# The begin of a one-core attention and MLP kernel: which engine issues the first loads, and in which order

## The chip, the cores and the metric

The kernel runs on one core of one Trainium2 chip. The metric is the device time of one execution in microseconds (us), the median over several runs. The profile of one execution stands beside it: a record of every instruction on the engines PE (TensorE: matmul products; PEld is its weight loads), DVE (VectorE), ACT (ScalarE), POOL (GpSimd) and SP (SyncE), and of every packet that the core's 16 DMA engines move. Transfers are issued by SP and ACT into hardware queues (q1 is SP's, q10 ACT's) and by POOL into a software queue (q0).

## What is computed

The reference is a linear attention with decay, followed by a two-layer MLP. `lam` holds eight numbers, one for each head.

```python
# q, k, v: (4, 8, 768, 64) float32; lam: (8,); block = 64
for b in range(nb):
    intra = (qb @ kb.T * Dmask) @ vb           # Dmask[i, j] = lam ** (i - j) for i >= j, else 0
    inter = (qb * lam_pow) @ kv_state
    out[:, :, sl] = intra + inter
    kv_state = lam_block * kv_state + (kb * rev_pow).T @ vb
x = out.transpose(0, 2, 1, 3).reshape(3072, 512)
h = x @ w_in                                    # w_in (512, 2048)
result = (h - tanh(h)) @ w_out                  # w_out (2048, 512)
```

The weights w_in and w_out come in with eight bytes for each number (the kernel sees them as I64) and are rounded to float32 on the chip.

## The kernel before

The sequence is cut into six groups of 128 positions, `g` = 0 to 5, and each group has one **chunk** for each of the four batches: chunk 0 to chunk 3 of group 0 are what the begin works on. A chunk's q, k and v are 256 KB each, 128 positions by 8 heads by 64 numbers, so a row in DRAM that lies together is 256 bytes. `load_natural` (L174, the transfers at L190) issues them.

The weight w_in is read in 16 **blocks** of 512 KB, `raw64`, (u, i) with u the quarter of the hidden layer and i the slice of 128 inputs. `load_weights` (L275) issues the loads into four buffers (`WAHEAD`), `weights` (L285) rounds a block: three ScalarE instructions (L353, L354, L355) read the raw block, and two of VectorE (L357, L358) finish it. When the third ScalarE instruction is done, the buffer is free for the block four places later. Blocks with i = 2 or 3 are loaded as two halves of 64 partitions (L271), the others as one transfer (L266).

The work of group 0 on a chunk b is, in order:

- `att_transpose` (L392): four transposes of q and four of k on TensorE, each set copied from PSUM by ScalarE (L394) as `qt` and `kt`.
- `att_scores` (L408): sixteen products `sp` of kt and qt; VectorE multiplies them by the decay mask `whole` (L415) into `ss`.
- `first_out` (L459): the products `op` of v and `ss`. For the chunks 0 and 1 together, and for 2 and 3 together, ScalarE then copies the tokens `xt` (L466, `first_tokens`).
- `att_decay` (L438): VectorE scales the chunk's k in place; `kv_products` (L447): the products for the running state.

`up_plain` (L903) then yields the products `h` of the MLP's first layer, from xt and a rounded block, four products at a step of the generator. `steps(unit, 2)` runs two steps, those of one block for 256 tokens.

The mask `whole` needs lam: `few` (L97) loads the eight numbers, VectorE widens them (L129), TensorE transposes them into `rows` (L132), VectorE copies them to `lam_all` (L133) and makes the mask by eight scans (L121). `idle_products(n)` (L105) writes n products of a zero tile that nobody reads: fillers that keep TensorE at work. Each of them shows as two passes in the profile, as does every product of this kernel.

The order of the begin is written out by hand, and `tc.keep_in_program_order` pins it on each engine. SP issues q of all four chunks, v of the chunks 0 and 1 and the blocks 1, 2 and 3; ACT issues k of the chunks 0 and 1; POOL issues lam, block 0, and k and v of the chunks 2 and 3. Two of POOL's transfers are held: `held(op, engine)` makes the next transfer of that engine wait for an instruction `op`. Block 0 waits for a scan of the mask (`begun`), and v of chunk 2 for the masked scores of chunk 0. From block 4 on, SP issues w_in, each block when its buffer is free.

Of the kernel before, what the change touches and what calls it, by code (L numbers as in the profile page):

```python
# [24 lines left out]
def kernel(  # L25
# [32 lines left out]
    nc = tc.nc  # L58
    B, H, S, D = q.shape
# [3 lines left out]
    KI = DM // 128  # L63
# [3 lines left out]
    NU = DFF // 512  # L67
# [26 lines left out]
    fwd = const.tile([128, NP, BLK], F32)  # L94
    nc.vector.memset(fwd[:, 0, :], 0.0)
    few = const.tile([H, 1], F32, name="few")
    nc.gpsimd.dma_start(out=few, in_=bass.AP(tensor=lam.tensor, offset=lam.offset, ap=[[1, H], [1, 1]]))  # L97
    make_identity(nc, ident)

    idle = psum.tile([128, 512], F32, name="idle", tag="w", bufs=1)  # L100
# [1 line left out]
    def idle_products(n, first=False):  # L102

        for _ in range(n):
            op = nc.tensor.matmul(out=idle[:, 0:128], lhsT=fwd[:, 0, :], rhs=fwd[:, 0, :], start=True, stop=True)  # L105
            if not first:
                tc.keep_in_program_order(op)
# [20 lines left out]
    few_wide = xpool.tile([H, BLK], F32, name="few_wide", tag="xt1")  # L128
    tc.keep_in_program_order(nc.vector.tensor_copy(few_wide, few.to_broadcast([H, BLK])))  # L129
    rows = psum.tile([128, 512], F32, name="rows", tag="z", bufs=1)[:, 0:H]  # L130
    idle_products(8, True)
    tc.keep_in_program_order(nc.tensor.transpose(out=rows, in_=few_wide, identity=ident[0:H, 0:H]))  # L132
    tc.keep_in_program_order(nc.vector.tensor_copy(lam_all, rows))  # L133


    begun = scans(range(NP), ident)
# [37 lines left out]
    def load_natural(g, b, names):  # L174
        for name, src, bufs in (("q", q, 2), ("k", k, 3), ("v", v, 4)):
            if name in names:
                if (g, b, name) in ((0, 2, "q"), (0, 3, "q"), (0, 3, "k")):
                    x = opool.tile([128, H, D], F32, name=f"{name}_nat", tag="o")
                else:
                    x = (qpool if name == "q" else io).tile([128, H, D], F32, name=f"{name}_nat", tag=name, bufs=bufs)  # L180
                rows = src[b, :, ts(g, BLK), :].rearrange("h s d -> s h d")
                if name == "q":
                    parts = [(nc.sync, x, rows)]
                elif g == 0:
                    parts = [(nc.gpsimd if b > 1 else nc.scalar if name == "k" else nc.sync, x, rows)]
                else:
                    parts = [(nc.sync, x[ts(1 - t, HALF), 4:8], rows[ts(t, HALF), 4:8]) for t in range(2)]
                    parts.insert(0, (nc.sync, x[:, 0:4], rows[:, 0:4]))
                for eng, to, of in parts:
                    op = tc.keep_in_program_order(eng.dma_start(out=to, in_=of))  # L190
                    if begin.get(eng) is not None:
                        wait_for(op, begin.pop(eng))
                raw[g, b][name] = x
# [67 lines left out]
    def load_block(eng, dst, kind, n, m, first=False):  # L261

        if kind == "out":
            tied(first, eng.dma_start(out=dst, in_=moe_w_out[ts(m * KH + n, 128), :].rearrange("k (a n) -> k a n", a=2)))
        elif m < 2:
            op = tied(first, eng.dma_start(out=dst, in_=w_in_u[ts(m, 128), :, ts(n, 256)]))  # L266
            if begin.get(eng) is not None:
                wait_for(op, begin.pop(eng))
        else:
            for j in range(2):  # L270
                op = tied(first, eng.dma_start(out=dst[ts(1 - j, 64)], in_=w_in_u[ts(2 * m + j, 64), :, ts(n, 256)]))  # L271
                if begin.get(eng) is not None:
                    wait_for(op, begin.pop(eng))

    def load_weights(n):  # L275

        while ready["loaded"] < min(n, ready["may"]):
            if moe_w_in.dtype != F32:
                raw64 = stage.tile([128, 2, 256], I64, name="raw64", tag="raw64", bufs=WAHEAD)
                block = blocks[ready["loaded"]]  # L280
                load_block(nc.gpsimd if ready["loaded"] in (0, *range(NU * KI, NU * KI + 4)) else nc.sync, raw64, *block, True)
                wraw[ready["loaded"]] = raw64
            ready["loaded"] += 1

    def weights(n):  # L285

        while ready["done"] < min(n, len(blocks)):
            at_ = ready["done"]
            load_weights(at_ + WAHEAD)
            kind, n_, m = blocks[at_]  # L290
            if kind == "out" and m == 0:
                pair[n_] = pair_tiles(n_)
            w = w1[n_][:, m] if kind == "in" else pair[n_][m][:, 0:2]
            if at_ in wraw:
                round_block(w, wraw.pop(at_), at_ < 3 * KI)
            else:
                load_block(nc.gpsimd, w, kind, n_, m)
            ready["done"] += 1
# [102 lines left out]
    def att_scores(g, bs):  # L401
        for b in bs:
            qt, kt, _ = tr[g, b]
            if g == 0:
                sp = [bank("sp", "att", 4).rearrange("s (p i) -> s p i", p=NP) for _ in range(2)]
                for p in range(NP):
                    for j in range(2):
                        tied(True, nc.tensor.matmul(out=sp[j][:, p, :], lhsT=kt[ts(j, 64), p, :],  # L408
                                                    rhs=qt[ts(j, 64), p, :], start=True, stop=True))
                if b % 2 == 0:  # L410
                    sc[0, "half"] = wst.tile([128, 8, 256], F32, name="ss", tag="w").rearrange(
                        "s (b j x) c -> s b j (x c)", b=2, j=2).rearrange("s b j (p i) -> s b j p i", p=NP)
                ss = sc[0, "half"][:, b % 2]
                for j in range(2):
                    op = tied(True, nc.vector.tensor_tensor(ss[:, j], sp[j], whole[:, j], op=AL.mult))  # L415
                sc[g, b] = ss
                continue

            sp = [bank("sp", "att", 4)[:, 0:6 * HALF].rearrange("s (x i) -> s x i", x=6) for _ in range(2)]
            for p in (0, 2, 1, 3):  # L420
                x, r = p % 2, p // 2
                for j in range(2):
                    kj, qj = kt[ts(j, 64), p, :], qt[ts(j, 64), p, :]

                    k0, k1 = (kj[:, ts(t if r == 0 or g >= GB else 1 - t, HALF)] for t in range(2))
                    tied(g != 1, nc.tensor.matmul(out=sp[j][ts(r, HALF), x:3 + p:2 + p - x, :], lhsT=k0,  # L426
                                                  rhs=qj.rearrange("d (t i) -> d t i", t=2), start=True, stop=True))
                    tied(g != 1, nc.tensor.matmul(out=sp[j][ts(1 - r, HALF), 2 + p, :], lhsT=k1,  # L428
                                                  rhs=qj[:, HALF:BLK], start=True, stop=True))
            ss = work.tile([128, 2, 6, HALF], F32, name="ss", tag="ss")  # L430
            for j in range(2):
                op = tied(g != 1, nc.vector.tensor_tensor(ss[:, j], sp[j], mask[:, j], op=AL.mult))
            sc[g, b] = ss
        return op

    def att_decay(g, b):
        kp = raw[g, b]["k"].rearrange("s (p j) d -> s p j d", j=2)
        return tied(g != 1, nc.vector.tensor_tensor(kp, kp, bwd if g > 0 else bwd_first, op=AL.mult))  # L438
# [525 lines left out]
    def steps(it, n):  # L964
        for _ in range(n):
            next(it)


    def held(op, *engines):
        begin.clear()  # L970
        begin.update({eng: op for eng in engines})

    def more_raw(n):
        ready["may"] = n
        load_weights(n)

    held(begun, nc.gpsimd)
    more_raw(1)
    more_raw(2)
    load_natural(0, 2, "q")  # L980
    more_raw(3)
    load_natural(0, 2, "k")
    att_transpose(0, (0,))
    idle_products(4)
    held(att_scores(0, (0,)), nc.gpsimd)
    load_natural(0, 2, "v")
    load_natural(0, 3, "qkv")
    more_raw(4)
    ready["may"] = len(blocks)
    att_decay(0, 0)  # L990
    idle_products(1)
    att_transpose(0, (1,))
    idle_products(4)
    att_scores(0, (1,))
    first_out(0)
    weights(1)
    att_decay(0, 1)
    idle_products(5)
    first_out(1)
    first_tokens(0)  # L1000
    idle_products(2)
    att_transpose(0, (2,))
    weights(2)
    unit = up_plain(0, [(i, c + 10 * a) for c in (11, 12) for i in range(KI) for a in range(2)])
    steps(unit, 2)
    att_scores(0, (2,))
    kv = kv_products(0, (0, 1))
    weights(3)
    att_decay(0, 2)
    att_transpose(0, (3,))  # L1010
    steps(unit, 2)
    first_out(2)
    weights(4)
    att_scores(0, (3,))
    att_decay(0, 3)
    steps(unit, 2)
    first_out(3)
    first_tokens(1)
    first_state((0, 1), kv)
# [185 lines left out]
```

## Time and profile before

| What | Value |
|---|---|
| median of 3 runs | 658.95 us (658.14 to 660.87) |
| profiled execution, its own time | 660.13 us |
| its span, from the first to the last instruction | 658.3 us |
| PE busy | 649.2 us (99%) |
| DVE busy | 471.1 us (72%) |
| ACT busy | 244.4 us (37%) |
| POOL busy | 204.9 us (31%) |
| DMA moved | 125.78 MB, mean 191 GB/s |
| issue to landing: q of chunk 0, lam, block 0 | 4.1 us, 5.3 us, 8.3 us |

The span is 1.8 us shorter than the execution's own time. The profile's views name a group of instructions by its line in the kernel, its engine, its operation and the tiles that it writes and reads. The timeline merges neighbours of one kind into a row: start, duration, engine, line, operation, tiles, shape, count, and in brackets how long the engine had been idle before and who ended the wait. The table by stages gives for each stretch of time how long each engine was busy. The DMA view gives for a stretch the packets and megabytes of each queue, and the median time from an issue to its landing.

### The profile page before, as it was taken

What the parts mean: (1) busy time and instruction counts of PE and PEld (TensorE: products, weight loads), DVE (VectorE), ACT (ScalarE), POOL (GpSimd) and SP (SyncE); (2) the same over time, 40 slices, a digit from 0 to 9 for tenths busy, and PEclk for the clock granted to TensorE, in tenths of its full rate; (3) what the DMA queues carried; (4) which work ended last, traced back from release to release, by engine and by line L of the source; (5) the groups of instructions that cost most, each with busy time, mean ns of one, the idle gap of its engine ahead of it and who ended that gap; (6) DMA issues with size and microseconds to landing.
All of it is one profiled execution on the core that took longest, in us unless ns stands there. A gap on an engine that the chain in (4) does not pass through costs nothing. (4 is left out here: it accounts for less than half of the span.)

```text
span 658.3 us, 14826 instructions
## 1 busy us (share of the span) xinstructions
PE 649.2 (99%) x5761; PEld 595.1 (90%) x5761; DVE 471.1 (72%) x895; ACT 244.4 (37%) x485; POOL 204.9 (31%) x353
## 2 busy tenths in 40 slices
PE   8999999999999999999999999999999999999998
PEld 7788888888888999988989988999998899998897
DVE  3556989968878895678786658798468697466663
ACT  2676964722321223532213443213353223263210
POOL 3000125777123335202334401244411254400241
PEclk9999999999999999999999999999999999999999
DMA  9929976996759758957656966676967476721274
GB/s 207 226 95 203 261 225 208 374 295 197 198 119 232 222 183 247 221 107 175 196 188 195 249 127 151 148 237 207 244 129 147 128 245 224 228 75 32 88 245 165
DMA packets 156215, 125.78 MB, mean 191 GB/s; under 512 B 126977, under 2 KB 129281, under 8 KB 156145
## 3 DMA queue, kind: packets, MB, share of 16 engines
q0 software_dynamic: 27056, 88.04, 43.1%
q1 hardware_dynamic: 127008, 36.27, 26.3%
q8 instruction: 46, 0.75, 0.5%
q10 hardware_dynamic: 2080, 0.52, 0.4%
q14 instruction: 25, 0.20, 0.1%
HBM read 103.81 MB, written 20.97 MB: 190 GB/s over the span
## 5 line engine op out<-in xcount | busy, mean ns | idle before, releaser
L752 POOL DMA_DIRECT2D wb<-fine x148 | 79.8, 539 | 190.9 <-PE y L794 66.8
L851 ACT ACTIVATE q<-y 128x128 f32<-128x128 f32 x96 | 26.6, 277 | 142.8 <-PE y L847 141.8
L847 PE MATMUL y<-wb,g 128*128 128x128 f32 x456 | 60.4, 277 | 0.0
L903 PE MATMUL h<-xt,w 128*128 128x256 f32 x256 | 58.3, 383 | 0.3 <-DVE w L358 0.3
L847 PEld LDWEIGHTS y<-wb,g 128*128 128x128 f32 x456 | 55.1, 192 | 0.9 <-issue 0.2
L903 PEld LDWEIGHTS h<-xt,w 128*128 128x128 f32 x256 | 47.4, 190 | 7.9 <-DVE w L358 1.3
L617 ACT ACTIVATE th<-g 128x512 f32<-128x512 f32 x40 | 25.2, 630 | 66.6 <-DVE g L635 50.7
L755 POOL DMA_DIRECT2D wb<-factors x44 | 23.7, 541 | 83.1 <-PE y L794 50.8
L609 PE MATMUL y<-xt,w 128*128 128x256 f32 x192 | 45.0, 379 | 0.0
L618 DVE TENSOR_TENSOR g<-g,th 128x512 f32<-128x512 f32 x40 | 27.6, 691 | 20.7 <-ACT th L617 20.7
L609 PEld LDWEIGHTS y<-xt,w 128*128 128x128 f32 x192 | 36.4, 190 | 5.1 <-ACT g L626 0.2
L847 PE MATMUL zw<-wb,g 128*128 128x128 f32 x304 | 40.3, 275 | 0.0
L609 PE MATMUL y<-tt,ws 128*128 128x256 f32 x160 | 37.8, 379 | 0.0
L609 PE MATMUL y<-tt,w 128*128 128x256 f32 x160 | 37.8, 379 | 0.0
L609 PE MATMUL z<-xt,ws 128*128 128x256 f32 x160 | 37.8, 379 | 0.0
L794 PE MATMUL y<-wb,g 128*128 128x256 f32 x160 | 37.3, 379 | 0.0
L847 PEld LDWEIGHTS zw<-wb,g 128*128 128x128 f32 x304 | 37.0, 192 | 0.2 <-DVE g L853 0.2
L794 PE MATMUL w<-wb,g 128*128 128x256 f32 x160 | 35.4, 379 | 0.0
L794 PEld LDWEIGHTS w<-wb,g 128*128 128x128 f32 x160 | 30.4, 190 | 4.1
L609 PEld LDWEIGHTS z<-xt,ws 128*128 128x128 f32 x160 | 30.4, 190 | 4.1
L794 PEld LDWEIGHTS y<-wb,g 128*128 128x128 f32 x160 | 30.4, 190 | 4.1
L609 PEld LDWEIGHTS y<-tt,w 128*128 128x128 f32 x160 | 30.3, 190 | 4.2
(217 smaller groups left out, 1465.9 us busy)
## 6 DMA issues: line engine op xcount, KB each, us to landing
wb<-fine POOLq DMA_DIRECT2D x148, 256.0 KB, 3.6
wb<-factors POOLq DMA_DIRECT2D x44, 256.0 KB, 4.5
wb<-fine_in POOLq DMA_DIRECT2D x36, 256.0 KB, 4.4
raw<-in_moe_w_out_dram SPq DMA_DIRECT2D x12, 512.0 KB, 5.4
rest<-fine POOLq DMA_DIRECT2D x20, 256.0 KB, 4.5
raw<-in_moe_w_in_dram SPq DMA_DIRECT2D x16, 256.0 KB, 7.5
fine<-f POOLq DMA_DIRECT2D x16, 256.0 KB, 5.0
q_blk<-in_q_dram SPq DMA_DIRECT2D x128, 32.0 KB, 3.2
```

The costliest lines, as they stand in the source:

```text
L609: nc.tensor.matmul(out=t[:, m, :], lhsT=wt[:, kt, ts(m, 128)], rhs=x[:, kt, :], start=first and m == 0 and kt == 0, stop=kt == 1, skip_gro ...
L617: nc.scalar.activation(th, src, AF.Tanh)
L618: nc.vector.tensor_tensor(dst(c), src, th, op=AL.subtract)
L752: nc.gpsimd.dma_start(out=t.rearrange("p m c -> p (m c)"), in_=fine[TWICE.index(n_), SUB.index(x_)].rearrange("p u c -> p (u c)"))
L755: nc.gpsimd.dma_start(out=t, in_=factors[XAT[FACT[n_][1]]][:, 2 * x_:2 * x_ + 2, :])
L794: nc.tensor.matmul(out=t[:, m, :], lhsT=a[:, u, kt, ts(m, 128)], rhs=wb[:, kt, :], start=first and u == 0 and m == 0 and kt == 0, stop=u = ...
L847: tied(x == STEPS[-1], nc.tensor.matmul(out=dst, lhsT=a[:, u, :], rhs=wb[:, ts(u, 128)], start=x in (1, 2) and u == 0, stop=u == NU - 1, s ...
L851: nc.scalar.activation(keep, dst, AF.Copy)
L903: tied(u == 0, nc.tensor.matmul(out=hm[c][:, m, :], lhsT=w1[u][:, i, a, ts(m, 128)], rhs=xt[0, t][:, i, :], start=m == 0 and i == 0, stop= ...
```

## The change

`few` is loaded by ScalarE, ahead of its two loads of k. Both holds are gone. POOL issues the first four blocks of w_in instead of block 0 alone (`range(KI)`, KI is 4), and between them k and v of the chunks 2 and 3, all written ahead of the first transposes. SP keeps q of all chunks, and v of the chunks 0 and 1. The fillers are divided anew: 6 before `rows` and 3 behind it instead of 8 before; none instead of 1 behind the first scores; 3 instead of 5 and 3 instead of 2 around the second `first_out`; 3 new ones ahead of the last. The first two steps of `up_plain` move ahead of the transposes of chunk 2, block 1 is rounded ahead of those, `kv_products` stands later, and block 3 is rounded behind the scores of chunk 3.

```diff
-    nc.gpsimd.dma_start(out=few, in_=bass.AP(tensor=lam.tensor, ...
+    nc.scalar.dma_start(out=few, in_=bass.AP(tensor=lam.tensor, ...
...
-    idle_products(8, True)
+    idle_products(6, True)
     tc.keep_in_program_order(nc.tensor.transpose(out=rows, in_=few_wide, identity=ident[0:H, 0:H]))
     tc.keep_in_program_order(nc.vector.tensor_copy(lam_all, rows))
+    idle_products(3)
...
-                load_block(nc.gpsimd if ready["loaded"] in (0, *range(NU * KI, NU * KI + 4)) else nc.sync, raw64, *block, True)
+                load_block(nc.gpsimd if ready["loaded"] in (*range(KI), *range(NU * KI, NU * KI + 4)) else nc.sync, raw64, *block, True)
...
-    held(begun, nc.gpsimd)
-    more_raw(1)
     more_raw(2)
-    load_natural(0, 2, "q")
+    load_natural(0, 2, "qk")
     more_raw(3)
-    load_natural(0, 2, "k")
+    load_natural(0, 2, "v")
+    load_natural(0, 3, "qk")
+    more_raw(4)
+    load_natural(0, 3, "v")
+    ready["may"] = len(blocks)
     att_transpose(0, (0,))
     idle_products(4)
-    held(att_scores(0, (0,)), nc.gpsimd)
-    load_natural(0, 2, "v")
-    load_natural(0, 3, "qkv")
-    more_raw(4)
-    ready["may"] = len(blocks)
+    att_scores(0, (0,))
     att_decay(0, 0)
-    idle_products(1)
     att_transpose(0, (1,))
     idle_products(4)
     att_scores(0, (1,))
     first_out(0)
     weights(1)
     att_decay(0, 1)
-    idle_products(5)
+    idle_products(3)
     first_out(1)
     first_tokens(0)
-    idle_products(2)
-    att_transpose(0, (2,))
-    weights(2)
+    idle_products(3)
     unit = up_plain(0, [(i, c + 10 * a) for c in (11, 12) for i in range(KI) for a in range(2)])
     steps(unit, 2)
+    weights(2)
+    att_transpose(0, (2,))
+    steps(unit, 2)
     att_scores(0, (2,))
-    kv = kv_products(0, (0, 1))
     weights(3)
     att_decay(0, 2)
+    kv = kv_products(0, (0, 1))
     att_transpose(0, (3,))
     steps(unit, 2)
     first_out(2)
-    weights(4)
     att_scores(0, (3,))
+    weights(4)
     att_decay(0, 3)
-    steps(unit, 2)
+    idle_products(3)
     first_out(3)
```

More of the change, by code (lines that the diff above doesn't have):

```diff
@@ L96 @@
     few = const.tile([H, 1], F32, name="few")
-    nc.gpsimd.dma_start(out=few, in_=bass.AP(tensor=lam.tensor, offset=lam.offset, ap=[[1, H], [1, 1]]))
+    nc.scalar.dma_start(out=few, in_=bass.AP(tensor=lam.tensor, offset=lam.offset, ap=[[1, H], [1, 1]]))
     make_identity(nc, ident)
@@ L1012 @@
     first_out(2)
+    att_scores(0, (3,))
     weights(4)
-    att_scores(0, (3,))
     att_decay(0, 3)
-    steps(unit, 2)
+    idle_products(3)
     first_out(3)
```

## The prediction

> **What bounds the kernel now.** I read the page first: its busy table and the PE row of the 40 slices.
>
> ```profile
> span 658.3 us, 14826 instructions
> ...
> PE 649.2 (99%) x5761; PEld 595.1 (90%) x5761; DVE 471.1 (72%) x895; ACT 244.4 (37%) x485; POOL 204.9 (31%) x353
> ...
> PE   8999999999999999999999999999999999999998
> ```
>
> TensorE is idle for only 9.1 us in all. The change touches the first 35 us alone, so I ask how far it shifts one marker: the end of the last L459 product of chunk 3. Next, the table by stages tells whether a shift lasts:
>
> ```profile
> 34.20:60.00 25.80, 25.80 (x145) 22.22 (x146) 13.34 (x24) 18.60 (x32) 0.00 (x0) 1.00 0.59 132
> 60.00:80.00 20.00, 19.74 (x182) 16.60 (x181) 19.18 (x45) 16.71 (x32) 2.28 (x4) 1.00 1.03 248
> ```
>
> The first two numbers behind each stretch are its length and PE's busy time: after the marker PE does not wait, so what is won or lost before it reaches the end. Third, the timeline of the begin (start, duration, engine, line; in brackets the idle time before):
>
> ```profile
> 1.06 3.78 PE L105 MATMUL idle<-fwd 128*128 128x128 f32 x16 [1.06 <-DVE fwd L95]
> 1.26 0.66 POOL L97 DMA_DIRECT2D few<-in_lam_dram  x1 [0.82 <-POOLq L1189]
> ...
> 6.94 0.24 PE L132 MATMUL rows<-ident,few_wide 8*128 8x8 f32 x1 [2.10 <-DVE few_wide L129]
> ...
> 8.02 1.06 PE L392 MATMUL tp<-ident,k_nat 128*128 128x128 f32 x4
> 8.22 0.76 POOL L266 DMA_DIRECT2D raw<-in_moe_w_in_dram  x1 [5.72 <-DVE whole L121]
> ...
> 10.71 2.08 PE L408 MATMUL sp<-qt,kt 64*128 64x128 f32 x16
> ...
> 14.91 1.16 PE L408 MATMUL sp<-qt,kt 64*128 64x128 f32 x16
> ...
> 18.34 1.09 PE L459 MATMUL op<-ss,v_nat 128*64 128x128 f32 x16
> ...
> 20.78 1.89 PE L903 MATMUL h<-xt,w 128*128 128x256 f32 x8
> ...
> 26.77 0.63 PE L392 MATMUL tp<-ident,k_nat 128*128 128x128 f32 x4 [1.33 <-DMA k_nat<-in_k_dram]
> ...
> 33.10 1.09 PE L459 MATMUL op<-ss,v_nat 128*64 128x128 f32 x16
> ```
>
> The marker is 33.10 + 1.09 = 34.19. Two PE waits stand before it: 2.10 us for lam and 1.33 us for chunk 3's k. The same L408 work takes 2.08 us at 10.71 and 1.16 us at 14.91: the PE clock opens in between (filler products stand 0.21 us apart before, 0.11 after). Last, the DMA view: from 2 to 28 us the engines are full, so order is all that can be won there, unless packets get larger.
>
> **Lam.** Lam is issued by POOL at 1.26 and lands 5.3 us later, at 6.55. On ScalarE it is the first transfer, at 0.74. Its latency lies between the quickest lone load on a hardware queue, 2.2 us (64 KB of k near 84 us), and q's first load, 4.1 us. It has nothing ahead of it, so I take 2.2: landed at 2.9. Then PE's six fillers bind (twelve passes of 0.21 from 1.06: 3.8) and `rows` runs at 3.9, not 6.94. With 4.1 it would be 5.2, and PE pauses over 1 us. Three new fillers take 6 x 0.21 = 1.3 us, to 5.3; they cost nothing, as k of chunk 0 lands at 5.53, and now about 0.48 us later, behind lam's issue on ScalarE: 6.0. Its transposes end at 7.0, not 9.08. The four fillers before the scores (8 x 0.21 = 1.7 us) end at 8.75, and the first scores begin there, not at 10.71: 2.0 us.
>
> **Clock.** PE works without a pause from 1.06. If the clock opens by 7, the fillers shrink, the scores start when kt is copied (7.75), last 1.16 and end at 8.9; if it opens late, they end at 8.75 + 2.08 = 10.8. I take the middle, 9.9, against 12.79 before: 2.9 us. The Trainium skill ("TensorE: Matmul & The Clock Gate", Part 1) has the clock open after a window of some 3.4 us of activity that runs free of the program; by it the end would be nearer 8.9. Part 4 adds that transposes do not count as activity, and so speaks for the late end; the opening at about 12.7, nearly 6 us after PE resumed, agrees with both.
>
> **Fillers and order.** From the first scores' end to the second L459 group took 18.34 - 12.79 = 5.55 us. One filler goes (0.26), five become three (4 passes of 0.14, of which some 0.4 stood in the way). So that group could start at 9.9 + 4.9 = 14.8, if its data is there. From it to the token copy is 1.09 + 0.7 us, then the first L903 products: about 16.9. Those now run ahead of chunk 2's transposes, so more lies between them and the marker: three L903 pairs 5.8, two transpose groups 2.1, two scores 2.3, kv 1.15, two L459 groups 2.2, three fillers 0.8, and 0.45 waiting for the last masked scores, which no product hides now: 14.8 us. Rounding fits: three ACT rows (0.68, 0.78, 0.76) and DVE's 0.69 make block 1 ready 3.0 us after the tokens, and PE gets there at 2.9. Block 3's later rounding is hidden by that last L459 group.
> Marker: 16.9 + 14.8 = 31.7, a gain of 2.5 us before late data.
>
> **Transfers.** POOL loses lam (0.66) and its two waits, so block 0 is issued at about 1.9, not 8.22. Ten issues of 0.5 to 0.9 us follow on POOL; only the last two wait, for blocks 0 and 1 to land, and nothing else is due on POOL before 70 us. SyncE loses five block issues and sends q of chunks 2 and 3 from 5.2. So POOL's queue now competes with chunk 1's q, k, v. The DMA view shows what that means. First 5 to 9 us, hardware queues alone; then 74 to 77, POOL's w_out blocks beside SyncE's natural loads (packets, MB, share):
>
> ```profile
> q1 hardware_dynamic: 2385, 0.61, 95.2%
> q10 hardware_dynamic: 1030, 0.26, 40.5%
> ```
> ```profile
> q0 software_dynamic: 219, 0.79, 77.6%
> q1 hardware_dynamic: 777, 0.19, 30.2%
> ```
>
> Alone, 256-byte packets move 0.87 MB in 4 us (0.22 MB/us); beside POOL's 3.6 KB packets 0.19 MB in 3 us (0.063), while POOL gets 0.26 MB/us. v's 64 KB parts show it too: landing takes 6.2 to 7.6 us at 71 to 82, 2.7 to 4.0 after 83.
>
> ```profile
> DMA to landing us min/median/max: 6.2/6.6/7.6
> ```
>
> The last v of chunk 1 needs 1.57 MB through the hardware queues; 0.76 MB have passed by 5.3. *Lower end:* POOL's packets come so late that nothing changes: 10.25, as now. *Upper end:* they come 3.5 us after the issue, at 5.4 (lam took 5.3 to land; block 0, issued 8.22, had no packet by 11.7), and then POOL's 3.1 MB keep the hardware queues at about 0.055 MB/us (0.045 beside k and v, from 21 to 25 us): 14 us later, 19.6. The trace has POOL transfers of both kinds (v of chunk 2, issued at 14.4, took 10.9 us), so I take the middle, 15.0: the L459 group waits 0.2 us. Block 0 now lands near 10, not 16.56; its rounding hides behind the scores. The 1.33 us stall for k of chunk 3 goes, as k is early in POOL's queue; late next is q of chunk 3, last on SyncE. All 5.24 MB pass by 5.3 + 4.5/0.22 = 25.8 at the old rate, by 21.9 at 0.27; its transposes are due near 24. I charge 0.3 us.
>
> **Sum.** 2.5 - 0.2 - 0.3 = 2.0 us. Profiled execution: 660.13 (span 658.3, 1.8 around it) becomes 658.1; against the shown median 658.95, which I use, 656.9.
>
> **Rivals.**
> *Clear road:* POOL's packets come late and the clock opens early. The L459 group starts near 13.8: 3.7 us gained, 655.2. For it: v of chunk 2 got its first packets over 6 us after its issue. Against: lam and block 0.
> *Starved v (slower):* POOL's large packets hold chunk 1's v to 19.6. Then the group starts at 19.7, the marker is 36.4, 2.2 us later: 661.2. It decides as soon as that v lands after 17.5. For it: the 74 to 77 row. Against: block transfers from POOL came in bursts with gaps (none between 18 and 21 us). The Trainium skill ("DMA: Bandwidth & Descriptors", Queues, rings and completion order) lets each DMA engine take turns between queues packet by packet, which favours large packets and so this rival; the row has about 3.5 small packets to one large, milder than one to one.
> *Late q:* v is in time, but the old rate of 0.22 MB/us holds; q of chunk 3 lands at 25.8, its transposes wait 1.8 us, and most of the gain is given back: 658.2.
> That the edit does not act is excluded: the compiled order shows POOL's transfers first and free of engine waits.
>
> **Chances.** Forecast 0.40, clear road 0.18, starved v 0.22, late q 0.20. A measurement tells about 0.5% (3.3 us) from no change. Below 655.65 lie most of the clear road and the forecast's edge, 0.21; above 662.25 the worst of starved v, 0.06; the rest, 0.73, is within. The range 654.6 to 661.0 leaves out half of each outer case.
>
> **What would show it.** `rows` at L132 near 3.9 with no PE wait (lam right); L408's first group ending by 9.9 (clock); the wait before the second L459 group naming v (starved) or none; transposes of chunk 3 waiting for q (late q); the marker near 32.2. A PE pause over 3 us anywhere before 20, with products 0.21 us apart behind it, would make all of this wrong.

## The result and the profile after

The changed kernel takes 669.73 us, the median of 5 runs (669.30 to 671.53); the kernel before takes 659.33 beside it (5 runs, 658.14 to 660.87). The ratio is 1.0161, with a 95% interval of 1.0139 to 1.0184: slower by about 10.4 us, where 656.9 was forecast and 661.0 was the upper end. The profiled execution took 669.47 us. Lines of the changed kernel stand one further down (L460 for L459, L393 for L392, and so on).

The page, at the places shown of before:

```profile
span 667.7 us, 14835 instructions
...
PE 649.8 (97%) x5765; PEld 595.1 (89%) x5765; DVE 471.7 (71%) x895; ACT 244.3 (37%) x485; POOL 208.1 (31%) x357
...
PE   4799999999999999999999999999999999999998
```

PE's busy time is nearly that of before (649.8 against 649.2), and the span is 9.4 us longer: what was added is idle time. Only the first two digits of the PE row fell, from 8 9 to 4 7. A slice is 16.7 us, so the loss lies before 34 us. The timeline of PE there:

```profile
3.92 0.27 PE L132 MATMUL rows<-ident,few_wide 8*128 8x8 f32 x1
...
7.35 1.16 PE L409 MATMUL sp<-qt,kt 64*128 64x128 f32 x16
11.25 0.63 PE L393 MATMUL tp<-ident,q_nat 128*128 128x128 f32 x4 [2.73 <-DMA q_nat<-in_q_dram]
21.66 1.08 PE L393 MATMUL tp<-ident,k_nat 128*128 128x128 f32 x4 [9.78 <-DMA k_nat<-in_k_dram]
...
26.18 1.09 PE L460 MATMUL op<-ss,v_nat 128*64 128x128 f32 x16
...
28.06 1.09 PE L460 MATMUL op<-ss,v_nat 128*64 128x128 f32 x16
...
43.01 1.67 PE L460 MATMUL op<-ss,v_nat 128*64 128x128 f32 x16
```

Up to 8.5 us the begin is faster than forecast: `rows` runs at 3.92, and the first scores end at 7.35 + 1.16 = 8.51. Then PE waits 2.73 us for q of chunk 1 and 9.78 us for k of chunk 1. The marker is 43.01 + 1.67 = 44.68, 10.49 later than the 34.19 of before.

The table by stages (length; busy time of PE, PEld, DVE, ACT, POOL; granted clock; DMA share; GB/s):

```profile
12.20:25.90 13.70, 4.24 (x26) 4.05 (x28) 0.00 (x0) 2.74 (x5) 0.91 (x1) 0.50 1.04 194
...
44.70:70.00 25.30, 25.25 (x142) 21.75 (x143) 13.32 (x23) 18.04 (x31) 0.00 (x0) 1.00 0.57 135
```

In the first of these stretches PE is idle most of the time and its clock is at half (0.50); the DMA engines are full at 194 GB/s. Behind the marker PE does not wait, as before, so the loss stays: 9.6 of the 10.5 us are still there when the last products of the kernel begin (657.63, against 648.07 before).

Why k of chunk 1 is late, the DMA view tells (packets, MB, share of 16 engines). First the stretch from 6 to 10 us, then that from 14 to 18:

```profile
q0 software_dynamic: 215, 0.78, 69.2%
q10 hardware_dynamic: 736, 0.19, 21.1%
q1 hardware_dynamic: 577, 0.15, 16.4%
```
```profile
q0 software_dynamic: 216, 0.71, 92.5%
q1 hardware_dynamic: 230, 0.06, 12.9%
q10 hardware_dynamic: 75, 0.02, 3.8%
```

POOL's queue q0 moves 0.7 to 0.8 MB in 4 us both times. The hardware queues move 0.34 MB in the first stretch and 0.08 in the second, 0.02 MB/us: one small packet of q1 (230) for each large one of q0 (216). K of chunk 1 was issued by ACT at 1.26 in the kernel before and landed at 7.95; now lam stands ahead of it, it is issued at 1.82 and lands at 21.52. After 6 us only 0.26 MB passed through q10 at all, 0.19 of them before 10: most of the 256 KB had come by then, and PE waited for the rest. POOL's packets came from 4.62 us on, and its last transfer landed at 23.29; k of chunk 1 landed at 21.52, v of chunk 1 at 24.34, q of chunk 2 at 25.46, all within 2.2 us of the time when POOL had no more to send. Not all that was caught waited so long: q of chunk 1 landed at 11.11. The Trainium skill ("DMA: Bandwidth & Descriptors", Why a DMA increments its semaphore by 16 and not by 1) says that a transfer is complete only when each of its DMA engines has finished its part; the trace agrees: of the sixteen updates of this transfer's semaphore the first came at 8.01, the fifteenth at 18.83 and the last at 21.52, so one late part held up the whole.

SP felt it too. Its two issues of q for the chunks 2 and 3, in the timeline of SP:

```profile
5.42 17.66 SPq L191 DMA_DIRECT2D q_nat<-in_q_dram  x2
```

Two such issues took 1.06 us at the start of the kernel; here they took 17.66.

### The profile page after: what moved, and what is told of

Read it like the earlier page. It is cut to its first block, busy times and chain, and to the rows that moved or that the text cites. A ratio compares the mean times of both kernels' runs of the same rounds, so it can differ in the third digit from the quotient of the medians.

```text
span 667.7 us, 14835 instructions
## 1 busy us (share of the span) xinstructions
PE 649.8 (97%) x5765; PEld 595.1 (89%) x5765; DVE 471.7 (71%) x895; ACT 244.3 (37%) x485; POOL 208.1 (31%) x357
```

## The experiments

The theory at this point (the expectations call it 'queue'): POOL's transfers start before chunk 1 has landed, and starve what is unfinished on a hardware queue until POOL's queue is empty. The rivals: too much data ahead of chunk 1 whoever issues it; the closed clock; the new order of PE's work.

**Lam alone.** The kernel before, with lam on ScalarE and the fillers 6 and 3, holds kept.

```diff
-    nc.gpsimd.dma_start(out=few, ...
+    nc.scalar.dma_start(out=few, ...
-    idle_products(8, True)
+    idle_products(6, True)
...
+    idle_products(3)
```

> The kernel before with lam first on ScalarE and the fillers 6 + 3 around rows; both holds stay, blocks 1 to 3 stay with SyncE. Theory 'queue' (POOL's 4 KB packets hold back what ScalarE and SyncE still have in flight; lam's place is harmless): k of chunk 1 lands near 8, rows runs near 3.9. The scan that releases block 0 now ends near 4.9, so POOL's packets arrive near 8, with some 0.15 MB of chunk 1's v still to come: the marker (end of the last L460/L459 group of chunk 3) between 31.5 and 35, against 34.2 before; ratio 0.996 to 1.001. Rival 'lam' (the load of lam ahead of k on ScalarE's queue is what delays k): k of chunk 1 lands near 20 as in the changed kernel, the marker is past 42, ratio over 1.01.

Measured 661.25 against 660.12, ratio 1.0017 (1.0007 to 1.0027). Chunk 1 is not late (its k lands at 8.46), and the second L460 group starts at 14.10, 4.2 us earlier than before. All of it is lost again at one row of PE's timeline:

```profile
25.07 0.63 PE L393 MATMUL tp<-ident,q_nat 128*128 128x128 f32 x4 [4.33 <-DMA q_nat<-in_q_dram]
```

Q of chunk 3, behind the blocks on SP, lands at 24.93. PE waits 4.33 us, the clock falls to half for 3.4 us, and the marker is 34.60, 0.4 later than before. The 4 us that lam's move gains are kept only if the transfers behind it come earlier too.

**Without the holds alone.** Lam stays on POOL; the two `held` calls of the kernel before go.

```diff
-    held(begun, nc.gpsimd)
...
-    held(att_scores(0, (0,)), nc.gpsimd)
+    att_scores(0, (0,))
```

> The kernel before without its two holds; lam stays with POOL, blocks 1 to 3 with SyncE. POOL then has 1.6 MB (block 0, k and v of chunks 2 and 3) ahead of it from about 2.6 us, half of the changed kernel's 3.1 MB. Theory 'queue': the slowest part of k of chunk 1 lands when POOL's queue runs dry, about 3 us after the first issue plus 1.6 MB at 0.2 MB/us: near 13 instead of 8, v of chunk 1 near 16 to 20; marker 35 to 40, ratio 1.002 to 1.009. Rival 'lam': k of chunk 1 lands near 8 and the ratio is 0.997 to 1.002, as lam is not on ScalarE.

Measured 659.09 against 660.12, ratio 0.9982 (0.9973 to 0.9992): not the loss that the theory of starvation expected. Starvation is there, but meets nothing that is due: v of chunk 0 lands at 15.43 and of chunk 1 at 16.32, with POOL's last at 15.33, and PE needs the second at 18.35. The marker is 33.09, 1.1 earlier.

**A hold put back.** The changed kernel with the first hold of before: POOL's first block waits for a scan of the mask, and is issued at 5.24, not 1.48.

```diff
+    held(begun, nc.gpsimd)
     more_raw(2)
```

> The changed kernel with one hold put back: POOL's first block waits for the first scan of the mask (near 4.9 instead of an issue at 1.5). All else as changed. Theory 'queue': POOL's packets arrive near 8.3 instead of 4.3; k of chunk 1 has landed by then (near 8), only the end of chunk 1's v (about 0.15 MB) is caught and lands between 14 and 25; PE's 9.8 us wait for k is gone; marker 33 to 40, ratio 0.998 to 1.009. Rival 'lam' or rival 'order' (the new order of steps and fillers costs the time): still a wait of about 10 us for k or the same ratio of 1.014 to 1.018.

Measured 665.8 against 660.12, ratio 1.0084 (1.0069 to 1.0099). All of the chunks 0 and 1 has landed by 10.15, k of chunk 1 at 8.54. Now q of chunk 2, issued by SP at 5.29, is caught; PE's timeline:

```profile
25.94 1.09 PE L393 MATMUL tp<-ident,q_nat 128*128 128x128 f32 x4 [8.93 <-DMA q_nat<-in_q_dram]
```

It lands at 25.80, and POOL's last at 25.42. So starving is shown, and which transfer it hits is set by what is open when POOL starts. The expectation had only the end of v caught; the marker is 41.70, outside its 33 to 40.

**The clock.** Fillers in place of idle time, while PE waits for chunk 1, so that the clock stays open. The first try:

```diff
+                if (g, b) == (0, 1):
+                    idle_products({"q": 10, "k": 41}[x])
```

> The changed kernel with 10 fillers ahead of chunk 1's q transposes and 41 ahead of its k transposes, in the time in which PE waited 2.7 and 9.8 us. They add no wait if the theory 'queue' is right, since k lands at 21.5 whatever PE does. What they tell is the share of the clock: in the changed kernel it is at half from 12.2 to 25.9. If the clock is a second cost, as theory 'queue' has it, the k transposes, four fillers and scores of chunk 1 take 1.1, 1.1 and 1.2 us less in sum about 2 us: marker near 42.5 instead of 44.7, ratio to before near 1.012. Rival 'clock' (the closed clock is the larger part of the loss): the ratio falls under 1.006.

Measured 672.61 against 660.12, ratio 1.0188 (1.0156 to 1.0220). It did not isolate the clock: k of chunk 1 landed at 23.57 here, PE still waited 3.33 us, and the clock closed behind that. So a second version, with 50 in place of 41:

> The changed kernel with 10 fillers ahead of chunk 1's q transposes and 50 ahead of its k transposes, so that PE works until about 22.4 and waits for k for under 1.5 us (41 fillers left it a wait of 3.3 us, and the clock closed again). If k lands at 21.5 to 23.6 again and the clock stays open, the k transposes, four fillers and the scores of chunk 1 take 0.6, 1.1 and 1.2 us instead of 1.1, 1.9 and 1.9: the marker stands some 2 us earlier behind the landing of k than the 23.2 us of the changed kernel (44.7 - 21.5). A time within 3 us of the changed kernel's tells that the closed clock is the smaller part of the loss; under 664 us that it is the larger.

K of chunk 1 landed at 21.29, and fillers ran until it came; PE's timeline:

```profile
10.94 11.33 PE L105 MATMUL idle<-fwd 128*128 128x128 f32 x100
22.11 0.60 PE L395 MATMUL tp<-ident,k_nat 128*128 128x128 f32 x4
...
41.45 1.67 PE L462 MATMUL op<-ss,v_nat 128*64 128x128 f32 x16
```

The clock stays open, the transposes take 0.60 and not 1.08 us, and the marker is 43.12, 1.56 earlier than the 44.68 of the changed kernel, although PE ran fillers for 0.8 us after k had landed. (Lines of this kernel stand two further down again.) One run took 668.02. The clock is the smaller part of the loss: 1.56 and 0.8 make some 2 us of 10, from a single run.

**The blocks back on SP.** The changed kernel with blocks 1 to 3 on SP as before: POOL sends 1.6 MB, unheld, in place of 3.1.

```diff
-  load_block(nc.gpsimd if ready["loaded"] in (*range(KI), ...) else nc.sync, ...)
+  load_block(nc.gpsimd if ready["loaded"] in (0, ...) else nc.sync, ...)
```

> The changed kernel with blocks 1 to 3 back on SyncE; POOL keeps block 0 and k and v of chunks 2 and 3 (1.6 MB), unheld and issued from 1.5. Theory 'queue': POOL's packets arrive near 4.3 as in the changed kernel, k of chunk 1 is caught, but POOL's last transfer lands near 14 instead of 23.3, and k and v of chunk 1 land with it: the wait for k is 2 to 6 us instead of 9.8; marker 35 to 39, ratio 1.002 to 1.008. Rival 'trickle' (what is caught moves on at a steady 0.02 to 0.06 MB/us and lands when its own bytes are through, whatever POOL still has): k of chunk 1 lands near 20 as in the changed kernel, ratio over 1.012.

Measured 665.59 against 659.58, ratio 1.0087 (1.0062 to 1.0112). PE's timeline:

```profile
15.81 1.09 PE L393 MATMUL tp<-ident,k_nat 128*128 128x128 f32 x4 [6.25 <-DMA k_nat<-in_k_dram]
```

K of chunk 1 lands at 15.67, with POOL's last transfers at 15.76 and 17.05: half the data on POOL ends the starving earlier. The marker is 37.77 + 1.67 = 39.44, a little later than expected.

**Lam back on POOL.** The changed kernel, with lam's load and the eight fillers of before. Lam's 32 bytes stand ahead of the blocks on POOL, which are then issued from 2.48, not 1.48.

```diff
-    nc.scalar.dma_start(out=few, ...
+    nc.gpsimd.dma_start(out=few, ...
...
-    idle_products(6, True)
+    idle_products(8, True)
...
-    idle_products(3)
```

> The changed kernel with lam back on POOL, and its 8 fillers ahead of rows. Lam's load takes POOL 0.66 us, so block 0 is issued near 2.5 instead of 1.5, as in no_holds, where k of chunk 1 still landed at 7.8. Theory 'queue': k of chunk 1 has just about passed when POOL's packets arrive near 5.3 and lands by 9; only v of chunk 1 and q of chunks 2 and 3 are caught, and land when POOL's 3.1 MB are through, near 23 to 24. PE then waits near 9 us ahead of the first or second L459 group instead of ahead of k's transposes: marker 40 to 43, ratio 1.008 to 1.014. Rival 'lam' (lam on ScalarE is what costs the time): ratio 1.000 or less.

Measured 666.42 against 659.58, ratio 1.0093 (1.0059 to 1.0127). K of chunk 1 lands at 7.83, as before. V of the chunks 0 and 1 is caught instead (lines stand here as in the kernel before):

```profile
17.74 1.98 PE L459 MATMUL op<-ss,v_nat 128*64 128x128 f32 x16 [2.71 <-DMA v_nat<-in_v_dram]
...
23.28 1.09 PE L459 MATMUL op<-ss,v_nat 128*64 128x128 f32 x16 [2.09 <-DMA v_nat<-in_v_dram]
```

It is the rival *starved v* in kind, and longer: v of chunk 0 lands at 17.60 and v of chunk 1 at 23.14, POOL's last at 22.68, and the marker is 41.44. Two things move at once here: POOL's first large packets come at 6.92, not 4.62, and k of chunk 1 is issued at 1.26, not 1.82, as lam is out of its way. Together they decide whether k is caught as well; the runs do not part them.

**Everything late on one queue.** The hold of the third experiment, and q of the chunks 2 and 3 moved from SP to POOL, in order of use: block 0, q and k of chunk 2, block 1, q and k of chunk 3, block 2, v of chunk 2, block 3, v of chunk 3.

```diff
-                    parts = [(nc.sync, x, rows)]
+                    parts = [(nc.gpsimd if g == 0 and b > 1 else nc.sync, x, rows)]
...
-    more_raw(2)
+    held(begun, nc.gpsimd)
+    more_raw(1)
     load_natural(0, 2, "qk")
+    more_raw(2)
+    load_natural(0, 3, "qk")
     more_raw(3)
     load_natural(0, 2, "v")
-    load_natural(0, 3, "qk")
     more_raw(4)
```

> The changed kernel with POOL's first block held to the first scan, as in after_hold_scan, and q of chunks 2 and 3 moved from SyncE to POOL, in order of use: block 0, q and k of chunk 2, block 1, q and k of chunk 3, block 2, v of chunk 2, block 3, v of chunk 3. Theory 'queue' (a transfer caught unfinished on a hardware queue lands only when POOL's queue runs dry; within POOL's queue transfers land in order): q, k, v of chunks 0 and 1 have landed by 10.2, nothing is caught, q of chunk 2 lands near 13 and q of chunk 3 near 18; the clock stays open; marker 30 to 32.5, ratio 0.993 to 0.998. Rival 'bandwidth' (the 5.2 MB of the begin end at the same time in any order, so the loss only moves): some wait of 2 us or more remains, on k or q of chunk 3 or on v; marker 34 or later, ratio 1.000 or more.

Nothing is caught, and PE goes through without a wait for data of the chunks:

```profile
13.70 1.09 PE L460 MATMUL op<-ss,v_nat 128*64 128x128 f32 x16
...
28.90 1.67 PE L460 MATMUL op<-ss,v_nat 128*64 128x128 f32 x16
```

The marker is 30.57, 3.6 earlier than before and 14.1 earlier than in the changed kernel, with the same instructions on PE. The time did not follow: 658.54 against 659.58, ratio 0.9981 (0.9958 to 1.0004). PE is 4.7 us ahead until 643, and then waits at the last products of the kernel (L890), for two of the last four transfers that POOL issues. The timeline of POOL:

```profile
638.45 0.54 POOL L756 DMA_DIRECT2D wb<-factors  x1 [0.35 <-PE y L848]
641.79 1.60 POOL L756 DMA_DIRECT2D wb<-factors  x3 [2.79 <-PE y L848]
```

Before, these four stand 0.89 us apart. The view names PE as the cause of the 2.79 us, but PE had not paused: POOL itself stood still. The trace has two more such stops of POOL, ahead of its transfers 151 and 250; this is ahead of 350 (counted from 0; the last is 352). An 8-KB instruction fetch of POOL stood right ahead of this one (638.3), and none ahead of the one at 250. So the stop goes either with a place in POOL's code or with a count of what it has sent.

**Which of the two.** 24 tiny memsets on POOL behind the begin's loads move its code, and not its count:

```diff
+    pad = const.tile([128, 8], F32, name="pad")
+    for _ in range(24):
+        tc.keep_in_program_order(nc.gpsimd.memset(pad, 0.0))
     att_transpose(0, (0,))
```

> The version with chunk 2's and 3's loads all on POOL in order of use kept its gain of 3.6 us at the marker until 648 us and then lost about 4 us, where POOL stood still for 2.8 us between the first and the second of its last four factor loads (638.45 to 641.79), right behind an 8-KB instruction fetch. Here 24 tiny memsets stand on POOL behind its loads of the begin; nothing else changes, and the number of POOL's transfers stays. Theory 'code': the stop belongs to a place in POOL's code; 24 instructions more move it about 12 loads forward, into slack. No stop between the last four loads (0.9 us apart), PE's wait for factors at the end gone, span 653 to 654.5, ratio 0.990 to 0.995. Rival 'count': the stop comes at a certain count of POOL's transfers (the 350th of 352, and before it the 250th, where 3.31 us stood in place of 0.89): it stays where it is, span 657.8, ratio 0.996 to 1.000.

Measured 658.74 against 659.81, ratio 0.9993 (0.9978 to 1.0007). POOL's fetch moved to 625.9, and the stop stayed ahead of transfer 350:

```profile
639.21 0.54 POOL L756 DMA_DIRECT2D wb<-factors  x1 [0.36 <-PE y L848]
642.55 1.59 POOL L756 DMA_DIRECT2D wb<-factors  x3 [2.80 <-PE y L848]
```

The code is excluded. The kernel before says the same: a fetch of this kind stands among its last four loads (at 645.0) without a stop. Once more without the memsets, to see whether the stop falls by chance:

> The same version as one_queue, one look more. Both 'code' and 'count' expect the stop between the first and the second of the last four factor loads again, 3.3 us apart, and span 657 to 658.5. If the stop falls by chance, or where an earlier execution left a counter, it stands somewhere else and the span is 653 to 655.

One run, 659.48, span 657.7: the stops are ahead of transfers 151, 250 and 350 again, and the last is again 3.33 us from issue to issue. Last, fewer transfers on POOL: the four stores of group 0 go over SP.

```diff
-        eng = nc.sync if g == NG - 1 else nc.gpsimd
+        eng = nc.sync if g in (0, NG - 1) else nc.gpsimd
```

> As above without the memsets, but the four stores of group 0 go out over SP instead of POOL, so that POOL has 348 transfers in place of 352. 'Count': the stop at the 350th never comes; no stop between the last four loads, span about 653.5, ratio 0.990 to 0.995. 'Code': POOL's code is 8 instructions shorter, the place of the stop comes 4 loads later in the program, which is at or behind the last one: as good. Only if the stop belongs to the last factor loads themselves (what the machine does at that time), does it stay here: ratio 0.996 to 1.000. The stores on SP hold a load of k behind them by some 20 us near 130 us; if that is needed there, PE waits near 150.

Measured 655.91 (655.62 to 656.50) against 659.81, ratio 0.9936 (0.9919 to 0.9952). The first two of POOL's last four loads (the others follow at 640.37 and 641.26), then PE's last products:

```profile
638.59 0.54 POOL L756 DMA_DIRECT2D wb<-factors  x1 [0.36 <-PE y L848]
639.48 0.54 POOL L756 DMA_DIRECT2D wb<-factors  x1 [0.36 <-PE zw L848]
```
```profile
643.48 7.19 PE L890 MATMUL end<-wb,g 128*128 128x256 f32 x48
```

No stop, no wait, span 653.9: this version beats both kernels, the kernel before by 0.6%. The load of k that the stores hold back on SP delays nothing that the waits show. The stop that was ahead of transfer 250 stands ahead of 256 here (3.45 us from issue to issue, 1.04 in the other). Four stores fewer moved it by six transfers, so it isn't transfers alone that are counted.

The stops are not new in these versions. The kernel before has them where they cost PE nothing, as its POOL timeline shows around transfer 168:

```profile
333.51 0.54 POOL L752 DMA_DIRECT2D wb<-fine  x1 [0.66 <-PE zw L847]
336.51 3.78 POOL L752 DMA_DIRECT2D wb<-fine  x7 [2.47 <-PE zw L847]
```

From issue to issue this takes 3.00 us, where the versions with one queue take 0.89 at the same place, and seven loads then follow without a pause: POOL was late, not what it waits for. Such a gap, over 2 us longer than in the other versions at the same place, stands ahead of transfer 168 and again of 268 in the kernel before, and of 167 and 266 in the changed kernel. That is 99 or 100 transfers and some 8,000 packets apart, as in the version with one queue, but at other places: there the third falls between the last four loads; in the kernel before, which has 347 transfers, a third at that distance would come behind the last.

## Why the prediction was wrong

- *Lam*: right. `rows` at 3.92 (forecast 3.9); the transposes of chunk 0 end at 6.53 (7.0).
- *Clock*: right in kind, too late in size. The clock opens at 5.4, ahead of the first transposes, so these ran fast too and the first scores end at 8.51 (taken: 9.9, bounds 8.9 to 10.8). The middle was too cautious; this is a gain of 1.4 more. Part of it is chance: in the versions that begin with the same fillers the clock opened anywhere from 4.3 to 6.1.
- *Fillers and order*: right. From the start of the second L459 group to the marker the forecast has 31.7 - 14.8 = 16.9 us; with no late data it takes 30.57 - 13.70 = 16.87 (the version with one queue). The marker of that version, 3.6 us earlier than before, is the *clear road* (3.7). The new order of PE's work is not the cause of the loss.
- *Transfers*: this step failed. It charged 0.2 us of waiting ahead of the second L459 group and 0.3 at chunk 3; PE waited 12.5 us, all for chunk 1. It failed in three places.
  - Its object. It asked when v of chunk 1 lands, and took k and q of that chunk as safe. K was caught, and that alone cost 9.78 us of waiting, q 2.73 more. The start was too late in the sum: POOL's first packets came 3.1 us after the first issue (1.48, not 1.9), at 4.62 and not 5.4; and k, which had needed until 7.95, was itself issued 0.56 later than before, behind lam. Q of chunk 2 was caught as well: it landed at 25.46, and PE, when nothing is late, asks for it at 17.23 (the version with one queue).
  - Its rate. The step took 0.055 to 0.063 MB/us for the hardware queues beside POOL, from the row at 74 to 77 us. From 14 to 18 us they got 0.02. V of chunk 1 landed at 24.34, later than the upper end of 19.6.
  - Its middle. Between 10.25 and 19.6 the step took 15.0. Its own rates gave more: 0.81 MB left from 5.4 on, at 0.055 to 0.063 MB/us, end at 18.3 to 20.1. The Trainium skill ("DMA: Bandwidth & Descriptors", Queues, rings and completion order) has each DMA engine take turns between the queues packet by packet; the prediction set it aside for the milder 3.5 to one of its row. Here the rows bear the rule out where POOL's queue is full: 239 packets of q1 to 238 of q0 from 10 to 14, 230 to 216 from 14 to 18. In the row at 74 to 77 POOL's share was 77.6%, here 89.8 and 92.5%: I take it that POOL's queue was less full in the row that I leaned on, which no run shows by itself.
- *Sum*: 14.1 us lie between the clear road's marker (30.57) and this one (44.68). Of these 2.73 + 9.78 = 12.5 are waiting, and the rest is about what the closed clock costs.
- *Starved v*, the slower rival (0.22), had the mechanism, and 661.2 was far too mild: it let POOL delay one transfer, to 19.6. V does land after its 17.5, but k decided sooner. The last paragraph's warning, a PE pause over 3 us before 20 and products at half clock behind it, is what happened.
- *Late q* is real as well: in the kernel with lam alone PE waits 4.33 us for q of chunk 3, and with the hold back 8.93 for q of chunk 2.

So the change took away what kept POOL's large packets behind the loads that PE needs first. It was not the missing holds alone: without them the kernel before lost nothing (ratio 0.9982). The loss came when POOL also began 1 us sooner, behind no lam, and had 3.1 MB to send in place of 1.6; either of these undone nearly halves it (1.0093 and 1.0087). The hold was also an order between queues.

## What to carry to other kernels

Two queues were not served by need here: while large packets ran on one, the last of the loads in rows of 256 bytes on another landed about when the first queue was empty (v of chunk 1 at 24.34 and POOL's last at 23.29; 16.32 and 15.33 without the holds). So put everything that is due at about the same time into one queue in order of use, and start a queue of large packets only when the small loads due first have landed. And when a gain at the begin is missing at the end, look where the lead is lost: here it was gone at the last four loads.

## What the runs showed of the hardware

- POOL stands still for some 2 us about every 100 transfers: ahead of its transfers 168 and 268 in the kernel before, 167 and 266 in the changed kernel, 151, 250 and 350 in three profiled executions of two versions that send the same, and 256 in the one with four stores fewer. The view charges the wait to other engines. The packets sent by the three stops are 11,488, 19,408 and 27,405, some 8,000 apart. What is counted, and from where, stays open.
- For part of the time SP's queue and POOL's moved packet for packet, whatever their size: 239 packets of 256 bytes to 238 of about 3.4 KB from 10 to 14 us of the changed kernel, 230 to 216 from 14 to 18. From 18 to 21 it was 542 to 157.
- Lam, 32 bytes as the first transfer on ScalarE, had landed about 1.4 us after its issue (0.74; VectorE widens it at 2.13); the quickest lone load that the prediction found took 2.2.
- An issue on SP is held up while its queue is starved: 17.66 us for two, 1.06 at the start.
